# A recurrent attention kernel: the output projection of 32 tokens on four column tiles instead of 40 on two, late rows projected at the end, rows turned by VectorE

## The chip, the cores and the metric

The kernel runs on one core of a Trainium2 chip. The metric is the time of one execution in microseconds (us): a median over runs, and the span of one profiled execution, from its first to its last instruction. Engines are written as the profile writes them: PE is TensorE's matmuls, PEld its weight loads, DVE is VectorE, ACT is ScalarE, POOL is GpSimd and SP is SyncE, which here issues most of the DMAs.

## What is computed

Two independent parts share the launch and write the two halves of each output row. Part A is a sliding, dilated attention over 2048 tokens; the change does not touch its code. Part B is a recurrence over 64 segments of 32 tokens, each with 8 memory rows ahead of it:

```python
mem = mem0
for s in range(n_seg):                       # 64 segments, one after the other
    xs = x[:, s * seg_len:(s + 1) * seg_len, :]
    h = jnp.concatenate([mem, xs], axis=1)   # 8 + 32 = 40 rows of 640
    q = jnp.einsum('btd,dhe->bhte', h, Wq)   # 32 heads of 192
    k = jnp.einsum('btd,dhe->bhte', h, Wk)
    v = jnp.einsum('btd,dhe->bhte', h, Wv)
    scores = jnp.einsum('bhqe,bhke->bhqk', q, k) * scale
    p = _softmax(jnp.where(mask[None, None], scores, -1000000000.0), axis=-1)
    o = jnp.einsum('bhqk,bhke->bhqe', p, v)
    o = jnp.einsum('bhte,hed->btd', o, Wo)
    mem = o[:, :M, :]                        # the next segment's memory
    outs.append(o[:, M:, :])
```

Only the first 8 rows of a segment's output feed the next segment. The four weight matrices are 640 x 6144 in bf16, and not all of them fit on the chip.

## The kernel before, in words

**Windows.** The 40 rows of a segment are handled as 32 + 8. The *main* rows are the 8 memory rows and the first 24 tokens. The last 8 tokens, the *late* rows, need no memory, so they are projected ahead of time, for four segments at once (32 rows, called `ahead`). A DRAM tile `XW` holds, for each segment, 32 main rows and 32 ahead rows (`copy_windows`, issue at L382, 26 DMAs). `load_x` (L469) brings the window of segment s + 1 into one of two tiles `HX` with a DMA transpose, at the start of segment s; a later copy (L657) overwrites the memory rows.

**Weights.** A weight unit is a 128-row slice of 1536 columns (Wq, Wk, Wv) or of two 640-column rows (Wo). 60 units stay in SBUF (`wres_*`), 24 units per segment are streamed from DRAM copies (`wcopy_*`) through six buffers of one tile (`wstream`, L417): 8 of Wk and 6 of Wv at 384 KB, 10 of Wo at 320 KB. All these DMAs are issued by SP, in one order; a fetch waits until PE has used the unit six places before it.

**Projections.** `project32` (L485) multiplies 32 rows by a unit as four matmuls of 384 columns, one on each 32-column tile of PE, so four run abreast. There are four groups g of eight heads each. Results go through a copy to bf16 (`to_sb`, L492), a turn by PE against an identity (`turn`, L498) and copies into `QT` and `KT`. Late rows of Wq, Wk and Wv are renewed each fourth segment, one k group and one v group and one q group in each segment (`RENEW`).

**Attention.** `scores` (L575) takes 16 matmuls per group; `softmax` and `put_p` run on DVE with the exponential on ACT (L582 to L600); `turn_p` (L610, L613) turns the probabilities and `mix` (L627) multiplies by the values with 32 matmuls on four row tiles. The result is copied into `OT` (L465), 40 tokens wide.

**Output.** `project_out` (L641) multiplies 64 columns of `OT` (40 of them tokens) with 320-column halves of a Wo unit: two matmuls abreast, 96 per segment, all summed into `Y`. At the end of a segment ACT copies `Y` to bf16 (L708), PE turns the 8 memory rows (`memory_rows`, L648 and L654), DVE copies them into the next `HX` (L657), and POOL issues two output DMAs (L716).

**Order.** `segment` (L659) writes out the order of PE by hand: projections of the next group stand between a group's scores and its use. The end of a segment is a loop-carried chain: the last `project_out`, the copy of `Y`, the memory rows, the next segment's first q projection. Instructions of the other engines, SP's among them, are put in order by a scheduler when the program is built.

PSUM has eight banks: three for projections, four single ones for everything that is turned, scored or mixed (`ps_x`), one for `Y`.

Of the kernel before, what the change touches and what calls it, by code (L numbers as in the profile page):

```python
# [23 lines left out]
def part_a(ctx, tc, A_x, A_wqkv, A_wo, out, ident, emit_loads):  # L24
# [239 lines left out]
    with tc.manual_schedule(engines={mybir.EngineType.PE, mybir.EngineType.DVE, mybir.EngineType.Activation}):  # L264
# [4 lines left out]
        for b in range(-1, n_blk):  # L269
# [13 lines left out]
STREAMED = {"k": ((2, 4), (2, 4), (0, 4), (0, 4)), "v": ((0, 4), (0, 4), (2,), (2,)),  # L283
            "o": (3, 5, 7, 10, 11, 13, 17, 18, 22, 23)}
# [3 lines left out]
LEAD_IN, PAD = 114, 4  # L288
# [9 lines left out]
def part_b(ctx, tc, B_x, B_mem0, B_Wq, B_Wk, B_Wv, B_Wo, out, ident, n_seg, pre, nbuf, mid):  # L298
# [6 lines left out]
    w_in = {m: w.rearrange("(dc p) h e -> p dc (h e)", p=128) for m, w in (("q", B_Wq), ("k", B_Wk), ("v", B_Wv))}  # L305
    wo_v = B_Wo.rearrange("h e d -> (h e) d").rearrange("(i k p) d -> p i k d", p=128, k=2)

    def unit_src(u):  # L310
        m, c, dc = u
        if m == "o":
            return wo_v[:, c]
        return w_in[m][:, dc, 1536 * c:1536 * c + 1536]

    def unit_cols(u):
        return 1280 if u[0] == "o" else 1536

    copied = {}

    def copy_streamed():

        order = [(m, g) for m, g in need]
        units = []
        for m, g in order:
            if m == "o":
                units += [("o", i, 0) for i in range(6 * g, 6 * g + 6) if i in STREAMED["o"]]
            else:
                units += [(m, g, dc) for dc in range(5) if m != "q" and dc in STREAMED[m][g]]
        for u in units:  # L330
            copied[u] = dpool.tile([128, unit_cols(u)], BF16, name="wcopy_%s%d_%d" % u)[:]
            nc.sync.dma_start(unit_tile(copied[u], u), unit_src(u))
# [4 lines left out]
    for m, g in need:  # L337
        if m == "o":
            resident += [("o", i, 0) for i in range(6 * g, 6 * g + 6) if i not in STREAMED["o"]]
        else:  # L340
            resident += [(m, g, dc) for dc in range(5) if m == "q" or dc not in STREAMED[m][g]]
    res, wait = {}, set()

    def unit_tile(t, u):
        v = t[:, 0:unit_cols(u)]
        return v.rearrange("p (k d) -> p k d", k=2) if u[0] == "o" else v

    def place_resident(pool, units):
        for u in units:
            res[u] = pool.tile([128, unit_cols(u)], BF16, name="wres_%s%d_%d" % u)[:]  # L350

    def load_resident(units, engs):
        for k, u in enumerate(units):
            engs[k % len(engs)].dma_start(unit_tile(res[u], u), unit_src(u))
# [8 lines left out]
    XW = dpool.tile([n_seg, 2 * SEG, Dm], BF16, name="xwindows")  # L363

    def copy_windows():

        rows = [(XW[0, 0:M], mem2[0:M]), (XW[0, M:SEG], x2[0:SEG - M])]
        for a, b in ((1, 49), (49, n_seg)):
            rows.append((XW[a:b, 0:SEG], x2[SEG * a - M:SEG * b - M].rearrange("(s n) d -> s n d", n=SEG)))
        groups = x2.rearrange("(t n) d -> t n d", n=SEG)[:, SEG - M:SEG]  # L370
        groups = groups.rearrange("(m k) n d -> k m n d", k=4)
        windows = XW[:].rearrange("(m k) n d -> k m n d", k=4)
        for r in range(4):
            for i in range(4):
                dst = windows[r][:, SEG + M * i:SEG + M * i + M]
                if i >= r:
                    rows.append((dst, groups[i]))
                else:
                    rows.append((dst[0:n_seg // 4 - 1], groups[i][1:n_seg // 4]))
                    rows.append((dst[n_seg // 4 - 1], groups[i][n_seg // 4 - 1]))  # L380
        for dst, src in rows:
            nc.sync.dma_start(dst, src)  # L382

    def emit_loads(turn_x):
        turn_x(1)
        load_resident(resident[:n_pre], [nc.sync])
        turn_x(2)
        copy_streamed()
        return copy_windows
# [7 lines left out]
    HXs = [xpool.tile([128, 5, 64], BF16, name=f"HX{i}") for i in range(2)]  # L397
# [5 lines left out]
    qk_sb = pool("b_qk", bufs=3)  # L403
# [3 lines left out]
    ps_x = pool("b_ps_x", bufs=4, space=PSUM)  # L407
# [3 lines left out]
    wait.update(resident[n_pre + len(early):])  # L411
# [8 lines left out]
    def get_unit(u):  # L420
        if u in fetched:
            return fetched.pop(u)
        if u in res:
            if u in wait:
                wait.remove(u)
                load_resident([u], [nc.sync])
            return res[u]
        return fetch(u)
# [9 lines left out]
    PADW = 64 - L  # L438
    QT = cpool.tile([128, 12 * L + PADW], BF16, name="QT")
    KT = cpool.tile([128, 4, 4, L], BF16, name="KT")  # L440
# [3 lines left out]
    OT = cpool.tile([128, 12 * L + PADW], BF16, name="OT")  # L444
    free = [cpool.tile([128, 3, 4, M], BF16, name=f"Lb{i}") for i in range(BLOCKS)]
    late = {}
    VW = 448
# [3 lines left out]
    nc.gpsimd.memset(KT[:], 0.0)  # L451
    for t in [QT, OT]:
        nc.gpsimd.memset(t[:, t.shape[1] - PADW:], 0.0)
    for t in LV + [Vst]:
        nc.gpsimd.memset(t[:, 192:256], 0.0)
# [4 lines left out]
               "QT": (S_, S_, S_, V_), "KT": (S_, S_, S_, S_), "V": (S_, V_, V_, S_), "LV": (V_, S_, S_, V_),  # L460
# [6 lines left out]
    def load_x(s):  # L467
        if s < n_seg:
            nc.sync.dma_start_transpose(HXs[s % 2][:], XW[s])  # L469

    def main(s):
        return HXs[s % 2][:, :, 0:SEG]

    def ahead(s):
        return HXs[s % 2][:, :, SEG:2 * SEG]
# [320 lines left out]
```

## Time and profile before

| | us |
|---|---|
| runs: median (lowest to highest) | 1974.92 (1973.56 to 1977.6) |
| the profiled execution's span | 1976.8 |
| first projection of Part B (L485) starts | 171.1 |
| copy of Y (L708) of the first and of the last segment starts | 217.5 and 1970.7 |
| one segment, mean of the 63 between these | 27.83 |
| PE busy, share of the span | 96% |
| DVE, ACT, POOL busy, share of the span | 52%, 47%, 13% |

The profile's page has six parts. Part 1 gives each engine's busy time. Part 2 cuts the span into 40 slices of 49.4 us and gives busy tenths, the granted PE clock, the mean busy share of the 16 DMA engines and the GB/s moved. Part 4 is the chain of work that ended last, followed back. Part 5 lists groups of instructions with their mean duration and what the engine waited for before them. Part 6 lists DMAs by source line, with the median time from issue to landing. Matmuls run abreast and are pipelined, so the duration of one (328 ns) is not the pace: the pace is read from the starts of successive ones in the timeline.

### The profile page before, as it was taken

The numbers are of one execution on the slowest core, as the hardware profiler recorded it, in microseconds if no ns is written. First come the engines' busy times: TensorE is split into PE (matmuls) and PEld (weight loads), VectorE is DVE, ScalarE is ACT, GpSimd is POOL, SyncE is SP. The second block draws the span as 40 slices with busy tenths as digits, with TensorE's granted clock in tenths as the row PEclk, the third lists the DMA queues.
The fourth block names the chain that finished last, engine by engine and source line by source line (L and its number), as shares of the span: only waits on it lengthen the run. The fifth ranks groups of instructions, "written<-read, shape, count | busy, mean of one in ns | idle before, by whom it ended". The sixth has DMA issues, their size and how long they took to land.

```text
span 1976.8 us, 99618 instructions
## 1 busy us (share of the span) xinstructions
PE 1890.8 (96%) x43006; PEld 1221.6 (62%) x43006; DVE 1032.1 (52%) x3431; ACT 927.4 (47%) x2963; POOL 262.3 (13%) x1070
## 2 busy tenths in 40 slices
PE   8998899999999999999999999999999999999998
PEld 5665566666666666666666666666666666666665
DVE  4885454455444554455445554455445554555454
ACT  3554344444444454444444454444444444444443
POOL 2001011111111111111111111111111111111111
PEclk9999999999999999999999999999999999999999
DMA  9936999999999999999999999999999999999997
GB/s 332 298 111 227 341 324 312 327 326 326 324 321 324 322 328 315 329 319 331 326 318 322 329 330 314 325 315 316 327 328 324 327 327 315 338 325 329 315 328 262
DMA packets 278203, 621.62 MB, mean 314 GB/s; under 512 B 62089, under 2 KB 72329, under 8 KB 277449
## 3 DMA queue, kind: packets, MB, share of 16 engines
q1 hardware_dynamic: 272258, 609.17, 91.3%
q8 instruction: 337, 5.52, 1.1%
q0 software_dynamic: 5504, 6.07, 1.0%
q14 instruction: 104, 0.85, 0.1%
HBM read 602.01 MB, written 19.27 MB: 314 GB/s over the span
## 4 chain that ended last, share of the span: by engine, by line
PE 67%; DMA 17%; ACT 7%; DVE 6%; issue 2%; SPq 0%; ACTq 0%; POOL 0%; POOLq 0%; DVEq 0%
PE acc L485 31%; PE Y L641 17%; DMA t<-wcopy_k 7%; PE pt L498 7%; DMA t<-wcopy_o 6%; DMA t<-wcopy_v 4%; PE Sps L575 3%; PE pq L95 3%; PE OTps L627 3%; DVE prod L151 1%; ACT sb L712 1%; ACT OT L708 1%; PE pt L610 1%; ACT KT L513 1%; ACT t L588 1%
## 5 line engine op out<-in xcount | busy, mean ns | idle before, releaser
L485 PEld LDWEIGHTS <-HX 128*32 128x32 bf16 x19380 | 467.1, 96 | 283.8 <-issue 54.5
L641 PEld LDWEIGHTS <-OT 128*64 128x64 bf16 x6144 | 317.8, 110 | 137.0 <-ACT OT L465 25.0
L485 PE MATMUL acc<-t,HX 128*32 128x384 bf16 x4524 | 342.9, 328 | 19.0 <-DMA t<-wcopy_k 9.3
L641 PE MATMUL Y<-wres_o,OT 128*64 128x320 bf16 x3584 | 331.2, 302 | 9.9 <-DVE OT L465 5.1
L485 PE MATMUL acc<-wres_q,HX 128*32 128x384 bf16 x6460 | 333.6, 328 | 1.1 <-issue 0.7
L492 ACT CAST sb<-acc 128x384 bf16<-128x384 f32 x448 | 210.1, 478 | 152.0 <-PE acc L485 132.4
L641 PE MATMUL Y<-t,OT 128*64 128x320 bf16 x2560 | 266.7, 301 | 10.4 <-DMA t<-wcopy_o 8.8
L485 PE MATMUL acc<-wres_v,HX 128*32 128x384 bf16 x4520 | 251.7, 327 | 0.7 <-DMA wres_v<-in_B_Wv_dram 0.7
L485 PE MATMUL acc<-wres_k,HX 128*32 128x384 bf16 x3876 | 224.6, 327 | 0.3 <-DVE sb L492 0.3
L588 ACT ACTIVATE t<-t 128x160 f32<-128x160 f32 x256 | 86.4, 338 | 288.5 <-DVE t L587 284.5
L498 PE MATMUL pt<-ident,sb 128*128 128x128 bf16 x1938 | 182.4, 221 | 8.5 <-ACT KT L513 0.9
L582 DVE SCALAR_TENSOR_TENSOR t<-Sps,mask 128x160 f32<-128x160 f32 x256 | 82.9, 324 | 178.5 <-PE Sps L575 173.2
L465 ACT CAST OT<-OTps 128x120 bf16<-128x120 f32 x512 | 108.6, 266 | 140.4 <-PE OTps L627 139.2
L498 PEld LDWEIGHTS <-sb 128*128 128x128 bf16 x1938 | 109.4, 97 | 87.0 <-ACT sb L492 20.5
L590 DVE TENSOR_REDUCE sm<-t 128x4 f32<-128x160 f32 x256 | 82.0, 320 | 130.9 <-ACT t L588 130.9
L465 DVE CAST OT<-OTps 128x120 bf16<-128x120 f32 x512 | 123.7, 272 | 46.1 <-PE OTps L627 45.8
L513 ACT CAST KT<-pt 128x256 bf16<-128x256 f32 (+1 forms) x323 | 109.1, 343 | 78.6 <-PE pt L498 78.1
L517 POOL COPY KT<-Lb 64x32 bf16<-64x32 bf16 x189 | 40.0, 212 | 788.2 <-PE Sps L575 656.9
L575 PEld LDWEIGHTS <-QT 128*64 128x64 bf16 x4096 | 98.4, 112 | 59.1 <-issue 52.2
L575 PE MATMUL Sps<-KT,QT 128*64 128x40 bf16 x4096 | 113.9, 187 | 5.6 <-ACT QT L507 2.6
L657 DVE CAST HX<-pt 128x40 bf16<-128x40 f32 x63 | 12.6, 200 | 179.5 <-PE pt L654 179.5
L600 DVE TENSOR_TENSOR P<-t,sm 128x128 bf16<-128x128 f32 (+1 forms) x512 | 100.2, 237 | 11.2
(91 smaller groups left out, 2130.8 us busy)
## 6 DMA issues: line engine op xcount, KB each, us to landing
t<-wcopy_o SPq DMA_DIRECT2D x640, 320.0 KB, 4.9
t<-wcopy_k SPq DMA_DIRECT2D x512, 384.0 KB, 5.3
t<-wcopy_v SPq DMA_DIRECT2D x384, 384.0 KB, 5.3
wres_q<-in_B_Wq_dram SPq DMA_DIRECT2D x20, 384.0 KB, 7.8
wres_v<-in_B_Wv_dram SPq DMA_DIRECT2D x14, 384.0 KB, 7.9
wres_k<-in_B_Wk_dram SPq DMA_DIRECT2D x12, 384.0 KB, 7.8
wres_o<-in_B_Wo_dram SPq DMA_DIRECT2D x14, 320.0 KB, 7.1
wcopy_o<-in_B_Wo_dram SPq DMA_DIRECT2D x10, 320.0 KB, 9.6
```

What stands on the lines that cost most here:

```text
L95: nc.tensor.matmul(pq[32 * d:32 * d + 32], lhsT=wcol[:, k, t, 4 * c + d, :], rhs=xTs[s][:, k, :], start=(k == 0), stop=(k == 4), tile_posi ...
L465: (S_ if copies["n"] % 2 else V_)(dst, src)
L485: nc.tensor.matmul(ps[n][32 * j:32 * j + 32, :], lhsT=X[:, dc, :], rhs=w[:, 384 * j:384 * j + 384], start=(dc == 0), stop=(dc == 4), tile_ ...
L492: copy(sb[:], p[:])
L498: nc.tensor.matmul(pt[:, k], lhsT=sb[:, 128 * c:128 * c + 128], rhs=ident, start=True, stop=True)
L513: copy(KT[:, :, 0:3:2, n0:n1].rearrange("p j c n -> p c j n"), src)
L575: nc.tensor.matmul(Sps[64 * g2:64 * g2 + 64, a, :], lhsT=QT[:, at:at + 64], rhs=KT[:, a, ((0, 1), (3, 2))[g2][part], :], start=(n == 0), s ...
L582: nc.vector.scalar_tensor_tensor(out=t1[:], in0=Sps[:], scalar=scale, in1=mask[:].unsqueeze(1).to_broadcast([128, 4, L]), op0=ALU.mult, op ...
L588: nc.scalar.activation(t1[:], t1[:], ACTF.Exp)
L590: nc.vector.tensor_reduce(out=sm[:], in_=t1[:], axis=AX.X, op=ALU.add)
L600: nc.vector.tensor_tensor(out=P[:, k, :, at:at + hi - lo], in0=t1[:, :, lo:hi], in1=sm[:].unsqueeze(2).to_broadcast([128, 4, hi - lo]), op ...
L641: nc.tensor.matmul(Y[64 * gv:64 * gv + 64, :], lhsT=OT[:, L * c:L * c + 64], rhs=w[:, n:n + 320], start=(i == 0 and r == 0), stop=(i == 23 ...
```

## The change

- **Windows and weights by quarters.** `XW` is laid out so that a segment's window is 128 rows: four quarters of the 640 columns times 32 rows. The row order of the Wq, Wk and Wv units is changed to fit (`(j dc f)`), resident units are loaded in blocks by four DMAs of 32 partitions each, and `copy_windows` issues 104 DMAs with 160-element runs where 26 stood. `load_x` becomes a plain DMA into a single tile `XS`, and DVE turns it in 32x32 blocks into `HX` (`turn_x`, placed after `put_p(s, 0)`).
- **Output of 32 tokens.** `project_out` takes 32 tokens, and puts the two chunks of a unit and its two column halves on four column tiles. The sums of the two chunks land on different partitions and are added in a new function `close`, which also turns the memory rows with DVE. POOL issues four output DMAs and one more per segment, that of the late rows.
- **Late rows.** The late 8 tokens' attention output is copied by POOL into `OL`, stored to a DRAM tile `late_o` at the end of each segment, and projected for all 64 segments after the last one (`project_late`): 16 loads of 384 KB back into the tiles of Wq, 1536 matmuls in two passes over Wo (streamed units are fetched twice), copies, and 64 DMAs of 8 rows.
- **Smaller attention products.** q's middle chunk is kept once for each of two heads, zero elsewhere, so `scores` takes 12 matmuls instead of 16; `mix` takes 24 instead of 32; `turn_p` takes 2 for each group.
- **Copies.** q's fills are three copies, k's are one; two of four k fills move from ACT to DVE; `mix` is followed by six copies instead of four. `ps_x` is two tiles of two banks.

```diff
+    w_in = {m: w.rearrange("(j dc f) h e -> j f dc (h e)", j=4, f=32) for m, w in (("q", B_Wq), ("k", B_Wk), ("v", B_Wv))}
...
+        n = len(units)
+        for j in (0, 2, 1, 3):
+            nc.sync.dma_start(t[32 * j:32 * j + 32].rearrange("p (n c) -> p n c", n=n),
+                              w_in[m][j, :, dc:dc + n, 1536 * g:1536 * g + 1536])
...
-    XW = dpool.tile([n_seg, 2 * SEG, Dm], BF16, name="xwindows")
+    XW = dpool.tile([n_seg, 4, SEG, 2, 160], BF16, name="xwindows")
+    late_o = dpool.tile([n_seg, 128, 48 * M], BF16, name="late_o")
...
-    ps_x = pool("b_ps_x", bufs=4, space=PSUM)
+    ps_x = pool("b_ps_x", bufs=2, space=PSUM)
...
-            nc.sync.dma_start_transpose(HXs[s % 2][:], XW[s])
+            nc.sync.dma_start(XS[:], XW[s].rearrange("j n w c -> (j n) (w c)"))
+
+    def turn_x(s):
+        if s < n_seg:
+            nc.vector.transpose(HXs[s % 2][:].rearrange("p w k n -> p (w k n)"), XS[:])
...
     def scores(g):
-        Sps = ps_x.tile([128, 4, L], FP32, tag="x")
-        for n in range(8):
-            a, part = n // 2, n % 2
+        Sps = bank()[:, 0:4 * L].rearrange("p (a n) -> p a n", n=L)
+        for a in range(4):
+            nc.tensor.matmul(Sps[:, a, :], lhsT=QT[:, QW * a:QW * a + 128], rhs=KT[:, a, 1, :], start=(a == 0), stop=False)
+        for a in range(4):
             for g2 in range(2):
...
     def mix(g, PT):
-        ps = [ps_x.tile([128, 3, L], FP32, tag="x", name=f"OTps{a}") for a in range(4)]
+        ps = [banks() for _ in range(2)]
...
-        for a in range(4):
-            evacuate(OT[:, 3 * L * a:3 * L * a + 3 * L], ps[a][:].rearrange("p k n -> p (k n)"))
+        for h, (first, second) in enumerate(((S_, V_), (V_, S_))):
+            p = ps[h][:, :, 0:4 * L].rearrange("p a (k n) -> p a k n", n=L)
+            O = OT[:, 2 * h:2 * h + 2]
+            first(O[:, :, 0:3:2, :], p[:, :, 0:2, :])
+            second(O[0:64, :, 1, :], p[0:64, :, 2, :])
+            second(O[64:128, :, 1, :], p[64:128, :, 3, :])
+        nc.gpsimd.tensor_copy(OL[:, :, 12 * g:12 * g + 12].rearrange("p n c -> p c n"),
+                              OT[:].rearrange("p a k n -> p (a k) n")[:, :, 32:L])
...
-                    nc.tensor.matmul(Y[64 * gv:64 * gv + 64, :], lhsT=OT[:, L * c:L * c + 64],
-                                     rhs=w[:, n:n + 320], start=(i == 0 and r == 0), stop=(i == 23 and r == 1),
-                                     tile_position=(0, 64 * gv))
+                    t = 32 * (2 * r + gv)
+                    nc.tensor.matmul(Y[t:t + 32].rearrange("p (b c) -> p b c", b=2),
+                                     lhsT=OT[:, c // 3, c % 3, 0:32], rhs=wide(w, r, gv),
+                                     start=(i == 0), stop=(i == 23), tile_position=(0, t))
...
+    def close(s, Y):
+        Ysb = OT[:].rearrange("p a k n -> p (a k n)")[:, 0:160]
+        odd = one.tile([128, 4, L], FP32, tag="t1", name="odd")[:].rearrange("p a n -> p (a n)")
+        for b, copy in ((0, V_), (1, S_)):
+            copy(odd[64 * b:64 * b + 64], Y[64:128, 160 * b:160 * b + 160])
+        for b in range(2):
+            nc.vector.tensor_tensor(Ysb[64 * b:64 * b + 64], Y[0:64, 160 * b:160 * b + 160],
+                                    odd[64 * b:64 * b + 64], op=ALU.add)
+        if s + 1 < n_seg:
+            nc.vector.transpose(XS[:, 0:160], Ysb)
+            nc.vector.tensor_copy(HXs[(s + 1) % 2][:, 0, :, 0:M],
+                                  XS[:, 0:160].rearrange("p (k n) -> p k n", n=SEG)[:, :, 0:M])
+        for j in range(4):
+            nc.gpsimd.dma_start(out2[SEG * s:SEG * s + SEG - M, Dm + 160 * j:Dm + 160 * j + 160],
+                                Ysb[32 * j + M:32 * j + SEG])
+        nc.gpsimd.dma_start(late_o[s], OL[:].rearrange("p n c -> p (n c)"))
...
         mix(3, PT[3])
         if not last:
             gl = (s + 1) % 4
-            ql = project32([ahead(s + 1)], "q", gl, range(0, 3))
+            ql = project32([ahead(s + 1)], "q", gl, slice(0, 2))
         project_out(Y, 3)
-        Ysb = OT[:, 0:320]
-        nc.scalar.copy(Ysb, Y[:])
+        close(s, Y)
...
+    def project_late():
+        dead = [("q", g, dc) for g in range(4) for dc in range(5)]
+        O = []
+        for b in range(16):
+            t = res[dead[b]].rearrange("p (i c) -> p i c", i=4)
+            nc.sync.dma_start(t, late_o[4 * b:4 * b + 4].rearrange("i p c -> p i c"))
+            O.append(res[dead[b]].rearrange("p (n c) -> p n c", c=48))
...
+        for part in ((0, 1, 2), (3,)):
+            for i in range(24):
+                w = get_unit(("o", i, 0))
+                for r in range(2):
+                    for m in part:
+                        for gv in range(2):
+                            for j in range(4):
+                                nc.tensor.matmul(sums[2 * m + gv][32 * j:32 * j + 32, 0:320],
+                                                 lhsT=O[4 * m + j][:, :, 2 * i + r],
+                                                 rhs=w[:, 640 * r + 320 * gv:640 * r + 320 * gv + 320],
+                                                 start=(i == 0 and r == 0), stop=(i == 23 and r == 1),
+                                                 tile_position=(0, 32 * j))
+            for m in part:
+                rows = res[dead[16 + m]][:, 0:640]
+                for gv, copy in ((0, S_), (1, V_)):
+                    copy(rows[:, 320 * gv:320 * gv + 320], sums[2 * m + gv][:, 0:320])
+                for k in range(16):
+                    r0 = SEG * (16 * m + k) + SEG - M
+                    (nc.sync, nc.scalar)[k % 2].dma_start(out2[r0:r0 + M, Dm:2 * Dm], rows[M * k:M * k + M])
```

More of the change, by code (lines that the diff above doesn't have):

```diff
@@ L287 @@
 BLOCKS = 18
[L288 removed]
+LEAD_IN = 114
 def next_start(m, g, s):
@@ L450, in part_b @@
     nc.gpsimd.memset(P[:], 0.0)
[L451 to L455, printed above, removed]
+    nc.gpsimd.memset(QT[:], 0.0)
     copies = {"n": 0}
@@ L603, in turn_p @@
     def turn_p(g):
[L605 to L606 removed]
+        pt = bank()[:, 0:256].rearrange("p (l n) -> p l n", l=2)
         for late in range(2):
[L608 to L614 removed]
@@ L615, in turn_p @@
-        PT = one.tile([128, 2, 2, L], BF16, tag="PT")
-        ENGINES["PT"][g](PT[:], pt[:].rearrange("p l (h n) -> p l h n", h=2)[:, :, :, 0:L])
+            nc.tensor.matmul(pt[:, late, :], lhsT=P[:, late].rearrange("p a n -> p (a n)"), rhs=ident,
+                             start=True, stop=True)
+        PT = one.tile([128, 2, 2 * L], BF16, tag="PT")
+        ENGINES["PT"][g](PT[:].rearrange("p l (h n) -> p l h n", h=2),
+                         pt.rearrange("p l (h n) -> p l h n", h=2)[:, :, :, 0:L])
```

257 lines of the change are left out of this document (136 added, 121 removed).

## The prediction

> **What bounds the kernel now.** First the page's slices, the queue shares and the issues, then the time windows (us from the start; span; busy time and count of PE, PEld, DVE, ACT, POOL; granted PE clock, DMA share, GB/s).
>
> ```profile
> PE   8998899999999999999999999999999999999998
> DMA  9936999999999999999999999999999999999997
> q1 hardware_dynamic: 272258, 609.17, 91.3%
> t<-wcopy_o SPq DMA_DIRECT2D x640, 320.0 KB, 4.9
> t<-wcopy_k SPq DMA_DIRECT2D x512, 384.0 KB, 5.3
> HX<-xwindows SPq DMA_TRANSPOSE x64, 5.2
> ```
>
> ```profile
> 497.00:1971.00 1474.00, 1426.36 (x33792) 923.65 (x33790) 749.64 (x2728) 697.41 (x2307) 199.86 (x843) 1.00 0.95 323
> 22.00:46.00 24.00, 23.00 (x403) 15.53 (x393) 15.73 (x17) 13.11 (x24) 0.00 (x0) 1.00 1.03 400
> 1055.60:1059.60 4.00, 4.00 (x95) 2.37 (x84) 1.56 (x5) 2.30 (x6) 0.21 (x1) 1.00 1.02 387
> 1036.50:1040.50 4.00, 4.00 (x108) 2.62 (x102) 2.96 (x11) 2.40 (x11) 0.00 (x0) 1.00 0.89 290
> 1024.50:1026.50 2.00, 2.00 (x36) 1.40 (x32) 0.14 (x1) 0.17 (x2) 0.00 (x0) 1.00 0.94 216
> ```
>
> The first window holds 53 segments: 27.8 us each, of which PE is busy 26.9 (1426.36 / 53). So PE bounds each segment, at full clock. But DMA stands close behind: a segment streams 14 x 384 KB + 10 x 320 KB = 8.78 MB, and 8.78 MB in 27.8 us is most of the 323 GB/s, with the DMA engines busy 0.95 of the time. What DMA can do at most is seen where many loads are queued: 400 GB/s while the resident weights load (22 to 46 us), 387 just after a segment's start, while in mid-segment, where PE sets the pace of new fetches, it is 290, and at the segment's end, where the DMA transpose of the window runs, 216. Next, what PE waits for in that stage, and the end of a segment in the timeline (start, us, engine, line).
>
> ```profile
> PE Y L641 <- DMA t<-wcopy_o: 6.3, 16, 1.0
> PE acc L485 <- DMA t<-wcopy_v: 6.2, 12, 1.4
> PE acc L485 <- DMA t<-wcopy_k: 5.5, 13, 1.0
> ```
>
> ```profile
> 1026.52 0.43 ACT L708 CAST OT<-Y 128x320 bf16<-128x320 f32 x1 [1.84 <-PE Y L641]
> ...
> 1027.00 0.39 PE L654 MATMUL pt<-ident,OT 128*64 128x8 bf16 x6
> ...
> 1027.42 0.20 DVE L657 CAST HX<-pt 128x40 bf16<-128x40 f32 x1 [2.78 <-PE pt L654]
> ...
> 1027.73 1.00 PE L485 MATMUL acc<-wres_q,HX 128*32 128x384 bf16 x20
> ...
> 1028.55 0.50 PE L485 MATMUL acc<-wres_k,HX 128*32 128x384 bf16 x8
> ```
>
> DMA waits are 18.0 us in 53 segments, 0.34 each; all PE idle is 47.6 us, 0.9 each. The chain from the copy of Y to the next q projection takes 1.21 us. And the last two lines give the pace of four matmuls abreast: 20 in 0.82 us, so 0.164 us for four of 384 columns.
>
> **Output projection: the gain.** Its 96 matmuls of 320 columns stay 96. Two abreast, 8 take 0.56 us in the timeline (two units at 1044.97 to 1045.53), so 0.14 us a pair, 48 pairs, 6.7 us. Four abreast cost 320/384 of 0.164 = 0.137 us for four; 24 of them take 3.3 us. **-3.4 us** a segment. The moving operand is read in two runs of 160 columns instead of one of 320; no row shows that. The bounds are 0 and, if the break counts as one more matmul, 96 x 0.01 (32 short ones of mix take 0.31) = 1.0; I take 0, since the other 320 columns are the same.
>
> **Scores, mix, turns of P.** 16 scores take 0.36 to 0.43 us now and 32 mixes 0.31; 16, 32 and 10 matmuls become 12, 24 and 8. A quarter of 4 x (0.36 + 0.31) is 0.67; but half of mix's streamed columns move into wider matmuls and the full-width scores no longer pair, so between 0 and -0.7; I take **-0.5**, the turns included.
>
> **End of segment.** Chain now 1.21 us. After: DVE copies half of Y (nearest: 0.27 for the 128x120 copy; 0.3), ACT the other half, and in the built order ACT waits for DVE there (0.3), two DVE adds from PSUM (0.32 each, as L582), a DVE turn of 160 columns (no row; between 0.20 of L657 and 0.35 of L587; 0.25), the copy into HX (0.2), five handovers at 0.05: 1.95. PE fills little of it (three steps of late q, 0.5, and one turn). **+0.75**, between +0.5 and +1.0.
>
> **New waits on PE.** (a) Shorter projections cover less. From scores(3) to the turn of its P, PE now takes 3.43 us (1046.08 to 1049.51), and DVE has P ready after 3.07. Six units lie between, losing 0.14 each: 2.6 us of cover, so PE waits 0.5. (b) Before the last output group, PE waits for the copies out of mix(3): three per engine (0.3 + 0.2 + 0.2) instead of two of 0.27, and only two steps of late q (0.33) beside them instead of three (0.49): +0.25. (c) q's and half of k's fills, the window's turn and the adds go to DVE: by its counts and these rows it goes from 14.1 us a segment (749.64 / 53) to about 19. Still under the period, so it costs by latency only. Together **+0.75**, between 0 and 1.3.
>
> **The window's load.** XS is one tile, so its load waits for the end of `close`; in the built order it stands on SP behind the six prefetched weights, and DVE's turn of it stands near the head of DVE's segment, ahead of the first softmax. Queued behind that turn on DVE: in every fourth segment (k group 0 renewed) the late k copy and q's fill, in the others the first softmax. Landing: 5.2 us after issue, as HX's transposes now. In the fourth-segment case PE wants the late k rows about 3.5 us after the segment's start, and gets them at 5.2 + 0.4 (turn) + 0.55 (copy) = 6.1: 2.6 lost. In the others scores(0) ends near 4.5 and its softmax starts near 5.6, but PE has q2 and v0 (1.6 us) ahead of the next need: near 0. Mean 2.6 / 4 = 0.65, partly beside DMA waits; **+0.5**, between 0 and 2.6.
>
> **DMA.** The transposes go; a plain window (82 KB), a store of late rows (98 KB) and output pieces come: about 9.0 MB a segment. At 387 GB/s 23.3 us, at 345 (the fuller windows) 26.1. With PE at about 26 it stays behind PE; I leave its 0.34 of waits as it is.
>
> Sum: 26.9 - 3.4 - 0.5 + 0.75 + 0.75 + 0.5 + idle of today 0.9 = **25.9 us** a segment, against 27.83: -1.93 x 64 = **-123.5**.
>
> **The late pass.** 1536 matmuls, 384 steps of four at 0.137 us = 52.6. Ahead of it 15 of the 16 loads of late rows (384 KB) pass through the last segment's queue beside its weights: 15 x 393 KB at 400 GB/s = 14.7 us; PE waits for those of the first pass, about 14. After it, in two rounds, the last 16 row DMAs and their landing (2.5 us for a 10 KB piece, about 5 in two rounds, behind the first pass's 48 DMAs): PE's end to the kernel's end about 10 instead of today's 6.1: +4. **+71.** The weight loads there read 32 columns at a stride of 96 bytes. Part A has strided ones (40 bytes), at 138 ns where contiguous ones of this width take 97; its matmul steps are 216 ns long and hide that, steps of 137 would not quite: 0 to +20, I take 0.
>
> **Start.** 104 window DMAs instead of 26, at 0.59 us an issue: 61 us from 93 on, so to about 155, where SP now has the window at 116 and the first stage waits for Part A's tiles until 148. Cover is Part A, which ends near 170. **+5**, between 0 and 25 (104 x 0.87, the pace of the 26 in all, ends at 184).
>
> Total on the profiled execution: 1976.8 - 123.5 + 71 + 5 = 1929. The runs' median is 2 us below that span: **1927 us**.
>
> **Rivals.** *The window's load decides (slower).* Place: DVE's turn at the head of each segment. If it lands behind all six prefetched weights, about 6 x 384 KB at 345 GB/s = 6.8 us after the segment's start, every softmax(0) starts 2.7 us late, of which q2 and v0 cover 1.1, and the fourth-segment case loses 4.2: (4.2 + 3 x 1.6) / 4 = 2.3 instead of 0.5. The period is then 27.7, and the time 1976.8 + 76 - 8 = 2045. It decides from a mean loss of 1.2 on, where 64 segments save no more than the 76 us of the late pass and the start. For it: the six weights are issued first. Against: today's transposes land after 5.2 with four or five loads ahead. 0.14.
>
> *DMA becomes the bound at today's rates.* 9.0 MB at 335 GB/s is 26.9 us: 1976.8 - 60 + 76 = 1993. For it: a share of 0.95 already. Against: 387 and 400 where the queue is full, and the transposes at 216 go. 0.12.
>
> *PE's new waits hide and the loads run at 387.* Period 24.2: 1976.8 - 232 + 76 = 1821; up to 1877 at 25.1. For it: waits on PE and DMA cover one another. [...] 0.19.
>
> Forecast (1885 to 1970): 0.55. Range: the lower end lies within the third rival, the upper takes in DMA at 335 and a slow start: **1850 to 2005**. About 0.2% (4 us) is what a measurement can tell from no change. Faster 0.74, same 0.04, slower 0.22.
>
> **What would show it.** Right: L691 at 0.137 us a step; copies of Y about 25.9 us apart; PE idle before the P turn of group 3 and at the late k turn; about 71 us from where the last segment would have ended. Wrong: DMA waits far above 0.34 us a segment (DMA is the bound), DVE's turn waiting on XS in all segments, late steps above 0.15 us, or a first projection after 185.

## The result: 29% slower, and the profile after

The changed kernel takes 2547.24 us (median of four runs, 2539.88 to 2555.83) where the kernel before took 1974.24 beside it: a ratio of 1.290, 95% interval 1.287 to 1.293. The prediction was 1927, range 1850 to 2005: wrong in sign and far outside its range. The profiled execution's span is 2554.0 us, 577.2 above that of before (1976.8). The page's slices, where before showed almost only nines for PE, for the granted clock and for DMA:

```profile
PE   8696777777777777777777777777777777777777
PEclk9798899989998989988999999999999999998899
DMA  9939878878787877777787777788777778787793
```

PE is below nine tenths in all slices but one, its clock is below nine tenths in 10 of the 40, and DMA, which stood at 0.95, has room. So neither of the two that were close to their limits before is the bound now. The time window of the loop, as shown before (span; busy of PE, PEld, DVE, ACT, POOL; granted clock, DMA share, GB/s):

```profile
540.00:2480.00 1940.00, 1484.57 (x31864) 832.68 (x31861) 1058.28 (x3694) 689.24 (x2152) 466.41 (x1374) 0.93 0.78 260
```

Copies of Y (L699) start at 260.4 and 2480.8, so a segment takes 35.24 us instead of 27.83. Of these PE is busy 27.0 and idle 8.2; it was idle 0.9. (PE does less work than before, but part of it at a lower granted clock, 0.93 in the mean where it was 1.00, so its busy time stays near 27.) Where the 577 us came from: the loop 63 x 7.41 = 467, the start 260.4 - 217.5 = 43, the tail from the last copy of Y 73.2 - 6.1 = 67.

Before, PE's longest waits in the loop were for DMA. Now (us in total, times, longest):

```profile
PE px L545 <- ACT QT L560: 101.2, 84, 4.3
PE px L545 <- ACT OT L676: 72.8, 69, 1.6
PE px L545 <- DVE Lb L494: 43.4, 27, 2.0
```

L545 is `turn`: PE turns projected rows and waits for copies out of PSUM. One such wait, in the timeline of the changed kernel (start, us, engine, line; in brackets the idle time before it and what ended it):

```profile
1009.68 0.34 PE L545 MATMUL px<-ident,sb 128*128 128x128 bf16 x3
...
1010.47 0.51 DVE L502 STREAM_TRANSPOSE HX<-XS 128x320 bf16<-128x320 bf16 x1 [2.58 <-DMA XS<-xwindows]
...
1011.79 0.29 DVE L564 CAST QT<-px 64x128 bf16<-64x128 f32 x1
...
1012.19 0.37 ACT L560 CAST QT<-px 128x256 bf16<-128x256 f32 x1 [2.31 <-DVE QT L564]
...
1012.62 0.33 PE L545 MATMUL px<-ident,sb 128*128 128x128 bf16 x3 [2.59 <-ACT QT L560]
```

Four things stand in one chain here. DVE waits 2.58 us for the window (XS) at the head of its segment. Behind it on DVE stand q1's two middle fills (L563, L564). ACT's outer fill of the same PSUM bank (L560) waits for DVE's to end. And PE's next turn, that of k1, waits for ACT's fill, although it writes the other bank of the two-bank tile, which no one is reading (by the order of calls of `bank()`, q1's turn takes the first bank of a tile here and k1's the second). The theories that follow take one of these links each: W the window, H the handover between two engines that read one bank, C the coupling of the two banks of a tile. G is the clock, O the order of the turns with two sb buffers.

### The profile page after: what moved, and what is told of

Same layout as the page of the kernel before. It is cut to its first block, busy times and chain, and to the rows that moved or that the text cites. A ratio compares the mean times of both kernels' runs of the same rounds, so it can differ in the third digit from the quotient of the medians.

```text
span 2554.0 us, 97114 instructions
## 1 busy us (share of the span) xinstructions
PE 1955.1 (77%) x40712; PEld 1129.0 (44%) x40712; DVE 1358.8 (53%) x4434; ACT 887.8 (35%) x2673; POOL 560.3 (22%) x1637
## 4 chain that ended last, share of the span: by engine, by line
PE 40%; DVE 23%; DMA 20%; ACT 8%; issue 5%; SPq 3%; ACTq 0%; DVEq 0%
PE acc L532 17%; DMA XS<-xwindows 11%; PE Y L691 8%; PE px L545 5%; DMA t<-wcopy_o 4%; SPq L409 3%; DVE t L628 3%; PE px L622 2%; ACT QT L560 2%; PE px L668 2%; DVE mx L632 2%; PE px L618 2%; DVE QT L564 2%; PE px L653 2%; DVE QT L563 2%
## 5 line engine op out<-in xcount | busy, mean ns | idle before, releaser
L545 PE MATMUL px<-ident,sb 128*128 128x128 bf16 x1938 | 220.6, 230 | 359.3 <-ACT QT L560 117.4
L545 PEld LDWEIGHTS <-sb 128*128 128x128 bf16 x1938 | 137.0, 100 | 481.3 <-issue 264.7
L677 POOL COPY OL<-OT 128x96 bf16<-128x96 bf16 x256 | 166.6, 651 | 725.7 <-ACT OT L676 519.8
L691 PE MATMUL Y<-wres_o,OT 128*32 128x320 bf16 x3584 | 238.2, 311 | 21.9 <-DVE OT L676 17.0
L563 POOL COPY QT<-Lb 64x32 bf16<-64x32 bf16 x252 | 51.4, 204 | 890.6 <-PE px L618 890.6
L691 PE MATMUL Y<-t,OT 128*32 128x320 bf16 x2560 | 218.2, 309 | 21.5 <-DVE OT L676 14.3
L691 PEld LDWEIGHTS <-OT 128*32 128x32 bf16 x6144 | 144.1, 97 | 170.3 <-DVE OT L676 55.6
L628 DVE SCALAR_TENSOR_TENSOR t<-px,mask 128x160 f32<-128x160 f32 x256 | 83.0, 324 | 250.2 <-PE px L622 248.6
L560 ACT CAST QT<-px 128x256 bf16<-128x256 f32 (+1 forms) x260 | 96.1, 370 | 254.8 <-DVE QT L564 250.5
L708 POOL DMA_DIRECT2D out_dram<-OT x256 | 128.0, 507 | 67.4 <-DVE OT L701 61.7
L502 DVE STREAM_TRANSPOSE HX<-XS 128x320 bf16<-128x320 bf16 x64 | 32.7, 511 | 167.4 <-DMA XS<-xwindows 167.4
L674 ACT CAST OT<-px 128x160 bf16<-128x160 f32 x256 | 74.1, 289 | 123.6 <-PE px L668 122.1
L674 DVE CAST OT<-px 128x160 bf16<-128x160 f32 x256 | 82.2, 321 | 60.3 <-PE px L668 59.7
```

The lines of the kernel that those rows point to most:

```text
L545: nc.tensor.matmul(pt[:, k], lhsT=sb[:, 128 * c:128 * c + 128], rhs=ident, start=True, stop=True)
L560: copy(Q[:, :, :, n0:n1].rearrange("p j c n -> p c j n"), src)
L563: copy(Qv[0:64, :, n0:n1], src[0:64])
L628: nc.vector.scalar_tensor_tensor(out=t1[:], in0=Sps, scalar=scale, in1=mask[:].unsqueeze(1).to_broadcast([128, 4, L]), op0=ALU.mult, op1=A ...
L674: first(O[:, :, 0:3:2, :], p[:, :, 0:2, :])
L677: nc.gpsimd.tensor_copy(OL[:, :, 12 * g:12 * g + 12].rearrange("p n c -> p c n"), OT[:].rearrange("p a k n -> p (a k) n")[:, :, 32:L])
```

## The experiments

All are edits of the changed kernel unless said otherwise; "a segment" is the mean distance of the copies of Y, 35.24 us in the changed kernel. Kernels whose loop is the same text differ by up to 0.5 us a segment (35.24, 35.20, 34.72 and 35.06 below), so smaller differences are not read.

**e1_window.** The window's load waits for less.

```diff
-            nc.vector.transpose(XS[:, 0:160], Ysb)
+            nc.vector.transpose(Vst[:, 0:160], Ysb)
...
         turn_x(s + 1)
+        load_x(s + 2)
```

> The changed kernel with a window load that waits for less: close turns the memory rows in the values' tile Vst instead of XS, and the load of the next window is issued right behind VectorE's turn, one segment earlier, so that XS is full long before its turn. Theory W (the window's load decides): VectorE waits 2.6 us a segment for XS, and QT and KT fills queue behind it, so 2.6 to 5 us a segment go: 2230 to 2380 us. Theory B (PSUM of two two-bank tiles decides) and theory O (order and the two sb buffers decide): the wait for XS is beside other waits, at most 0.5 us a segment goes: 2515 to 2547 us.

2399.65 us, 32.82 a segment: -2.4, just short of what W expected. The wait for XS is a third of the loss; two thirds stay.

**e2_ring.** One tile of four banks.

```diff
+    X4 = ps_x.tile([128, 4, 512], FP32, name="px")
...
+        return X4[:, n]
```

> The changed kernel with one tile of four PSUM banks in place of two tiles of two: single banks are handed out one after the other and each is free when its own reader is done. Theory B: PE's waits ahead of turns, of P turns and of mixes (L545, L653; 5.2 us a segment more than before) are half waits for the other bank of a tile, so 2 to 3 us a segment go: 2350 to 2420 us. Theories W and O: those waits are for copies of values not yet made, at most 0.5 us a segment goes: 2515 to 2547 us.

3035.06 us, 42.80 a segment: a miss for all, and the most telling run. The same spot in its timeline:

```profile
1037.30 0.33 PE L545 MATMUL px<-ident,sb 128*128 128x128 bf16 x3 [1.11 <-DVE t L628]
1039.04 0.33 PE L545 MATMUL px<-ident,sb 128*128 128x128 bf16 x3 [1.41 <-ACT QT L560]
```

Successive turns go to successive banks, yet each stands until the readers of the bank just before are done. So in this program a write waits for the readers of its whole tile, not of its bank, and more stands in one line with the larger tile: 42.80 us a segment with one tile of four banks, 35.24 with two of two. Theory B had taken the opposite as given. It becomes theory C.

**e3_nolate.** OL's copies, the store of OL and `project_late` left out.

> The changed kernel without the late rows: the copies into OL, the store of OL and the pass at the end are left out, so the last 8 rows of each segment's output are not written. All theories: the loop of 64 segments keeps its pace and only the pass (72 us) goes: about 2475 us. Were POOL's OL copies (0.65 us each) what OT or PE waits for, the pace would fall too: under 2440 us.

2454.04 us, 34.63 a segment. The pass is what goes; the loop falls by 0.6, about the scatter named above, so POOL's copies are not the cause.

**e4_sb3_order.** The same with three sb buffers and the turns where the kernel before has them.

```diff
-    qk_sb = pool("b_qk", bufs=2)
+    qk_sb = pool("b_qk", bufs=3)
...
-        both(tq[0])
         tq[1] = project_qk(s, "q", 1)
+        both(tq[0])
         both(tk[0])
...
-        both(tq[3])
         values(s, 2)
+        both(tq[3])
```

> As the run without late rows, and in the room that is free: three sb buffers as in the kernel before (the change has two) and with them the order of the kernel before, where q's first turn stands behind the second q projection and the last q turn behind the values of group 2. Theory O: PE stood at turns for sb copies and for QT and KT fills that the shorter distance laid open, 2 to 4 us a segment go: 2220 to 2350 us. Theories W and B: the waits move and stay as long: 2440 to 2475 us.

2596.59 us, 36.80 a segment, 2.2 more than e3: neither branch. From start to start PE loses 3.7 us a segment between successive turns (2.4 in e3) and 1.9 ahead of scores (0.2): with the turns close together their waits no longer lie apart, or so it seems; that was not followed. Theory O falls.

**e5_onehand.** One engine empties a bank.

```diff
-                fill_middle(V_, 0, 32, pt[:, 1])
+                fill_middle(S_, 0, 32, pt[:, 1])
...
-        for h, (first, second) in enumerate(((S_, V_), (V_, S_))):
+        for h, (first, second) in enumerate(((S_, S_), (V_, V_))):
...
-        for b, copy in ((0, V_), (1, S_)):
+        for b, copy in ((0, V_), (1, V_)):
```

> The changed kernel where one engine alone empties a PSUM bank: q's three fills all on ACT, each half of the mix by one engine (first ACT, second DVE), both halves of odd in close by DVE. Theory H (handovers: in the changed kernel's trace ACT's QT fill waits for DVE's, ACT's OT copy for DVE's, ACT's odd for DVE's, since readers of one bank on two engines run one after the other): the turns behind them wait less, 1.5 to 3 us a segment go: 2350 to 2450 us. Theory C (banks that are coupled because two share a tile): the waits stay nearly as long, 2500 to 2547 us.

2403.61 us, 32.87 a segment: -2.4, as H expected. But the edit does two things: it ends the handover, and it takes q's middle fills off DVE, in whose queue they stood behind the wait for the window. This run does not tell the two apart; e8 does in part.

**e6_single.** e3 with four single banks, and the mix of the kernel before (which needs no pairs).

```diff
-    ps_x = pool("b_ps_x", bufs=2, space=PSUM)
+    ps_x = pool("b_ps_x", bufs=4, space=PSUM)
...
-        ps = [banks() for _ in range(2)]
+        ps = [bank()[:, 0:3 * L].rearrange("p (k n) -> p k n", n=L) for a in range(4)]
```

> As the run without late rows (2454 us), with four single PSUM banks in place of two tiles of two, and with them the mix of the kernel before (32 matmuls, four copies of one bank each, values laid out in 448 columns). Theory C: in the ring of one tile the second of two turns stood for the first one's copies although it wrote another bank, and the trace of the changed kernel shows the same inside each tile of two; with single banks 3 to 5 us a segment go: 2130 to 2260 us. Theory H: only the mix's handovers go, 1 us a segment: about 2390 us. Theory W: 2440 us.

2116.39 us, 29.30 a segment: -5.3 against e3, more than C expected. The spot of the first timeline, in e6:

```profile
1006.05 0.61 PE L542 MATMUL px<-ident,sb 128*128 128x128 bf16 x6
...
1007.19 0.51 DVE L503 STREAM_TRANSPOSE HX<-XS 128x320 bf16<-128x320 bf16 x1 [2.99 <-DMA XS<-xwindows]
...
1008.91 0.37 ACT L557 CAST QT<-px 128x256 bf16<-128x256 f32 x1 [2.64 <-DVE QT L561]
```

DVE still waits for the window (2.99) and ACT still waits for DVE (2.64); but PE does both turns in one go (x6) and walks on into q2. The chain is there, and in this segment PE is no longer tied to it. Over all segments DVE waits for the window nearly as long as in the changed kernel (the changed kernel, then e6; us in total, times, longest):

```profile
DVE HX L502 <- DMA XS<-xwindows: 167.4, 61, 8.1
```

```profile
DVE HX L503 <- DMA XS<-xwindows: 146.8, 60, 8.0
```

In every fourth segment PE still stands for it, in another place. There the late rows of k0 are projected anew, their copy on DVE stands behind the window's turn, and PE waits for that copy:

```profile
1065.08 0.51 DVE L503 STREAM_TRANSPOSE HX<-XS 128x320 bf16<-128x320 bf16 x1 [4.59 <-DMA XS<-xwindows]
...
1066.09 0.51 PE L542 MATMUL px<-ident,sb 128*128 128x128 bf16 x6 [3.39 <-DVE sb L536]
```

Between 540 and 2000 us this happens 12 times, at 1.5 to 3.4 us and 2.1 in the mean, so 0.5 a segment. In the runs whose window comes early (e1, e10, e12) PE has no such wait.

**e11_pairs_oldmix.** e6 with the two tiles of two banks put back: the mix's four copies stay, only the tiles return.

```diff
+        two = [banks() for _ in range(2)]
+        ps = [two[a // 2][:, a % 2, 0:3 * L].rearrange("p (k n) -> p k n", n=L) for a in range(4)]
```

> As the run with single banks and the earlier mix (2116 us, no late rows), but with the two tiles of two banks put back; mix, its four copies and the values' layout stay those of the kernel before. Theory C (banks of one tile are coupled): the waits of turns and P turns come back, 2350 to 2454 us. Theory M (the changed mix with its six copies and handovers was what the run with single banks took away): 2116 to 2180 us.

2413.98 us, 33.84 a segment. So of e6's 5.3 us the tiles are 4.5 and the mix with its copies 0.8. C holds, M falls. (A mix takes two whole tiles, so a bank that is left over ahead of it goes unused; that is part of the 4.5 and was not measured by itself.) What PE waits for most in e11's loop, and the windows of e11 and of e6:

```profile
PE px L546 <- ACT QT L561: 70.6, 65, 3.1
```

```profile
540.00:2000.00 1460.00, 1135.61 (x26154) 641.18 (x26156) 777.64 (x2700) 490.51 (x1499) 226.69 (x855) 0.94 0.80 264
```

```profile
540.00:2000.00 1460.00, 1253.19 (x30308) 727.40 (x30300) 884.35 (x3128) 550.29 (x1735) 265.50 (x992) 0.98 0.90 306
```

In e6 no turn waits for a QT fill. Of the 4.5 us a segment, 3.4 are idle time of PE and the rest is busy time: the same matmuls take 26.3 instead of 25.1 us, the granted clock being 0.94 in e11 and 0.98 in e6.

**e7_warm.** Filler matmuls into Y's free bank at two of the waits.

```diff
         both(tq[1])
+        keep_warm(20)
         both(tk[1])
...
+        keep_warm(10)
         both(tk[2])
```

> The changed kernel with filler matmuls of the identity into Y's free bank where PE stands longest: 20 (about 1.8 us) ahead of k1's turns and 10 (0.9 us) ahead of k2's. They do nothing useful. Theory G (stalls also halve PE's clock for 3 us behind them: 0.924 granted): the clock rises to 0.96 or more and 1 to 2.5 us a segment go: 2390 to 2480 us. Rival (the halved clock lies beside waits that end as late anyway): the clock rises, the time stays or grows by up to 0.5 us a segment: 2545 to 2580 us.

```profile
540.00:2000.00 1460.00, 1152.60 (x25600) 690.65 (x25600) 806.87 (x2819) 524.70 (x1640) 356.49 (x1052) 0.97 0.80 262
```

2536.84 us, 34.75 a segment: the granted clock of the loop rises from 0.93 to 0.97 and the time falls by 10 us, between the two expected ranges and far nearer the rival's. The pace changes by no more than the scatter. So G is not the cause of the loss; that the halved clock lies mostly beside waits that end as late anyway fits this, and is not shown wait by wait.

**e8_window_onehand.** e1 and e5 together.

> The changed kernel with both the earlier window load and one engine for each bank. If handovers and the window cost one beside the other, the gains add: 2400 us less what one engine for each bank gives by itself, 2200 to 2300 us by theory H. If they cover the same waits, about 2380 to 2400 us.

2346.99 us, 31.93 a segment: -3.3, where the two alone sum to -4.8, and the time lies between the two expected ranges. They cover partly the same waits, being links of one chain. With the window early, one engine for each bank is worth 0.9 (e8 against e1), not much above the scatter; so 1.5 of e5's 2.4 are to be had only while the window is late.

**e10_fixed.** The whole kernel with single banks, e5's fills and odd, e1's window; the mix uses 64-column tiles for the middle chunk, so that values keep 384 columns.

```diff
+                for f in ((0, 0, 128, 0, 0), (1, 128, 64, 0, 0), (1, 192, 64, 64, L), (2, 256, 128, 0, L))]
```

> The whole changed kernel, late rows included, with three repairs: four single PSUM banks, with a mix whose middle chunk goes through 64-column tiles (32 matmuls, four copies of one bank each, values in 384 columns as changed); q's fills by ACT alone and odd by DVE alone; the window's load one segment earlier. If the gains add (338 us of single banks, 200 us of the other two): 2010 us, and if the two others only covered the same waits, 2210 us. The prediction's own sum had 1927 us; what is left above it is the start (43 us found, 5 taken) and waits that no repair here touches.

```profile
540.00:2000.00 1460.00, 1334.66 (x31459) 801.61 (x31458) 832.65 (x2885) 655.23 (x2165) 443.32 (x1291) 1.00 0.94 321
```

2132.43 us, 28.36 a segment, within what was expected. 415 us of the loss are repaired, and the clock is back to 1.00 in the loop by itself. It is still 8% slower than before.

**e12_mix448.** e10 with the mix of the kernel before, and OL stored in halves for room.

> As the run with three repairs (2132 us), but the mix of the kernel before: full 128-column tiles and values laid out in 448 columns, since the mix through 64-column tiles kept PE for 3.05 us a segment and this one for 1.52 in the run with single banks. The room comes from OL, stored twice a segment in halves. If PE sets the pace, 1.5 us a segment go: 2040 us. If DMA does (0.94 busy, 321 GB/s in the loop of the run with three repairs), the pace stops near 27.5 us a segment: 2075 us, and PE's waits for wcopy tiles grow.

2138.2 us, 28.50 a segment, above both expected times: PE has 1.6 us a segment less to do in the mix and the pace is the same. First lines of PE's waits in e12's loop; the second took the place of the work (it was 11.0 in e10), while the first, the end of the segment, stood in e10 as well:

```profile
PE acc L524 <- DVE HX L698: 33.6, 51, 0.7
PE Y L684 <- DMA t<-wcopy_o: 31.1, 51, 2.6
```

**e14_cut.** e12 without five of the 24 fetches of a segment.

```diff
-            w = get_unit(("o", i, 0))
+            w = get_unit(("o", 0 if i in (5, 10, 13, 18, 23) else i, 0))
```

> As the run with the mix of the kernel before and three repairs (2138 us, 28.5 us a segment), but the loop leaves out five of the ten fetches of Wo in a segment (1.64 of 9.15 MB): the units 5, 10, 13, 18 and 23 are multiplied with the resident unit 0, so the output is not that of the reference. If the transfers are the floor, the pace falls to PE's own, 26 to 26.9 us, and the total to 1970 to 2040 us. If PE's waits on copies are what is left, the pace stays within 0.4 us of 28.5 and the total above 2110 us.

2037.6 us, 26.99 a segment. The window of the loop of e12, then of e14:

```profile
540.00:2000.00 1460.00, 1285.07 (x31333) 748.77 (x31334) 820.35 (x2877) 644.88 (x2153) 461.54 (x1338) 0.98 0.93 320
```

```profile
540.00:1900.00 1360.00, 1227.92 (x30775) 726.04 (x30774) 803.42 (x2827) 633.88 (x2122) 453.82 (x1310) 1.00 0.84 276
```

With fewer bytes the pace falls by 1.5 us and DMA's share from 0.93 to 0.84. PE's DMA waits, 0.8 us a segment in e12, are gone, and its busy time falls by as much, from 25.1 to 24.4, with the granted clock back at 1.00. So under the repaired kernel the fetches are the floor, at 320 GB/s.

**e15_after_cut** and **e16_before_cut**: the same edit in the changed kernel and in the kernel before.

> The changed kernel with the same five fetches left out and unit 0 in their place (output not that of the reference). Theory C with its handovers (turns wait for copies): the transfers lie beside longer waits, 2500 to 2547 us. If the transfers cost the changed kernel time: under 2400 us.

> The kernel before with the same five fetches left out and unit 0 in their place (output not that of the reference). Its PE is busy 26.9 of 27.8 us and its DMA engines 0.94. If PE alone bounds it, only the DMA waits go (0.34 us a segment): 1950 to 1975 us. If the transfers bound it as much as PE, some 0.7 us or more: under 1935 us.

2480.65 us (34.36 a segment, -0.9) and 1935.97 us (27.34, -0.5; 2.1% faster than before, interval 1.8 to 2.4%). Both fell between the branches. In the changed kernel transfers cost little beside the 7.4 that a segment lost; the kernel before stood at PE and DMA together: without the fetches it gains more than its DMA waits (0.34) and less than 0.7.

**The start: e13_start, e17_few_issues, e18_128rows, e19_128rows_few.** e13 is e12 with every second window copy on ACT's queue; e17 copies the ahead rows with four DMAs instead of 88; e18 loads the resident units by one DMA of 128 partitions each; e19 is e17 and e18.

```diff
-        for j in (0, 2, 1, 3):
-            nc.sync.dma_start(t[32 * j:32 * j + 32].rearrange("p (n c) -> p n c", n=n),
-                              w_in[m][j, :, dc:dc + n, 1536 * g:1536 * g + 1536])
+        for i in range(n):
+            nc.sync.dma_start(t[:, 1536 * i:1536 * i + 1536], w_plain[m][:, dc + i, 1536 * g:1536 * g + 1536])
```

> As the run with the mix of the kernel before, with every second of the 104 window copies issued by ACT's queue instead of SP's. If the 43 us by which the start grew are SP's time to issue them (77 us from the first to the last in the changed kernel's trace), the first copy of Y comes 20 to 40 us earlier than in the run beside it and the total falls by as much. If they are the transfers themselves (16,000 packets of 320 bytes), it stays within 5 us.

> The changed kernel with the ahead rows of the windows copied in plain order, four DMAs where 88 stood, the same bytes in the same runs of 320 bytes (so the late rows are those of other tokens, and the output is not the reference's). If SP's 0.75 us for each issue made the start longer, the first copy of Y comes 25 to 45 us earlier than the changed kernel's 256 us, and the total is 2500 to 2525 us. If the packets did, it stays at 250 us or later.

> The changed kernel with the resident units of Wq, Wk and Wv loaded as before, by one DMA of 128 partitions each (so with the weights' rows in the order of the kernel before, and the output not the reference's). If the DMAs of 32 partitions are slow: 25 to 50 us moves near 400 instead of 220 GB/s, Part A's second transpose is issued near 52 us instead of 76, and the first copy of Y comes 15 to 30 us before the changed kernel's 256 us (SP's 77 us of window issues still stand ahead of the first window), the total near 2525 us. If not: 250 us or later.

> The same with the windows in 20 issues as well (late rows of other tokens). If these two are the whole start, the first projection begins near 171 us as in the kernel before and the first copy of Y near 220 us, the first segment being longer by the loop's own 7 us; total near 2510 us.

The expectations' 256 us is the moment at which DVE begins to wait for the first Y; its copy starts at 260.4. e13, a miss: 2189.72 us, copy at 308.6. Half of the issues now stand on ACT, which makes copies for Part A, and Part A's last matmul ends at 255.2 where it ended at 192.2 in e12; so it says nothing of SP. e17: 2544.13 us, copy at 254.7, 5.7 earlier, so it is not the issues that made most of the start: SP's window issues shrink from 78 to 23 us, but then the first projection (196.9) waits for Part A. e18: 2497.02 us, copy at 225.1. e19: 2503.26 us, copy at 219.5, against 217.5 before. Resident loads at 25 to 50 us, before, changed, and e18, each followed by the issue of Part A's transpose behind them:

```profile
25.00:50.00 25.00, 22.66 (x381) 15.10 (x373) 17.66 (x20) 13.15 (x25) 0.00 (x0) 1.00 1.03 398
```

```profile
51.68 6.61 SPq L49 DMA_TRANSPOSE xT<-in_A_x_dram  x1
```

```profile
25.00:50.00 25.00, 22.21 (x356) 14.40 (x349) 17.22 (x19) 12.46 (x24) 0.00 (x0) 1.00 1.04 220
```

```profile
75.90 8.49 SPq L49 DMA_TRANSPOSE xT<-in_A_x_dram  x1
```

```profile
25.00:50.00 25.00, 22.67 (x376) 14.68 (x368) 18.09 (x21) 13.15 (x25) 0.00 (x0) 1.00 1.03 401
```

```profile
51.35 8.00 SPq L49 DMA_TRANSPOSE xT<-in_A_x_dram  x1
```

With 32 partitions a DMA the loads run at 220 GB/s, with 128 at 398 and 401, the DMA engines being busy all the time in each (1.03 and 1.04) and a unit's row being 1536 columns in each; Part A's third transpose on SP (the expectations call it the second) comes 24 us late and Part A with it. That is 35 of the start's 43 us, and the window issues are another 6. Why loads of 32 partitions run at little more than half the rate of those of 128 was not shown.

## Why the prediction was wrong, step by step

- **Output projection, -3.4:** right in kind, a little less in size. Four abreast come 0.14 us apart (starts at 1031.52, 1031.66, 1031.80 in the changed kernel). From each start to the next, gaps counted up to 0.2 us, the stage (L641) took 6.9 us a segment before and 3.9 in e12 (L684): -3.0.
- **Scores, mix, turns of P, -0.5:** wrong in sign. From start to start the 12 scores take 1.7 us a segment in e12 where 16 took 1.4, and the changed mix 1.3 as before.
- **End of segment, +0.75:** right. From the first copy of Y to the next q projection 1003.02 to 1005.09: 2.07 instead of 1.21, so +0.86. The order was as told, ACT behind DVE.
- **New waits on PE, "together +0.75, between 0 and 1.3":** this is the step that failed. It took each bank as free when its own copies are done and asked only how long the copies are. The change says "`ps_x` is two tiles of two banks", and the step has no term for it, so it put the price at nothing: a turn waits for the readers of the tile, so the copies of q and k came to lie in PE's path. That alone is 4.5 us a segment (e11 against e6). Into the same path came q's fills on two engines, 2.4 (e5), of which 0.9 is left once the window is early (e8 against e1); the prediction had counted one handover, at the end of the segment.
- **The window's load, +0.5, between 0 and 2.6:** near its upper end, 2.4 (e1), and for a reason that the step did not see. DVE waited for XS in nearly every segment and not in each fourth, as the sign set for "wrong" said. But it does so in e6 nearly as long (167.4 and 146.8 us in all). There, with single banks, PE stands for it mainly where the step had put the loss: in every fourth segment, at the late rows of k, for 2.1 us instead of 2.6. The forecast's +0.5 was thus right for the path it followed; the rest of the 2.4 goes with the coupled banks. No run moved the window alone with single banks, so this split is read from waits.
- **DMA, waits unchanged at 0.34:** true of the changed kernel only because it is slow. Repaired, it meets the transfers at 28.5 us a segment, above the forecast's 25.9 and above the 26.9 of the rival "DMA becomes the bound at today's rates". Without five fetches (e14) it runs at 27.0, so 1.1 above the forecast, and not because of waits: PE is idle 2.6 us a segment there, where the forecast had 2.9 (0.75 + 0.75 + 0.5 + 0.9), but it is busy 24.4 where the forecast had 23.0 (26.9 - 3.4 - 0.5). So the first two terms, the savings on PE, were 1.4 too large together (e14's mix is that of the kernel before, which takes as long as the changed one).
- **The late pass, +71:** 67 measured, right; a step took 0.136 us, and the strided weight loads (140 ns) were hidden, as taken.
- **Start, +5, between 0 and 25:** 43. The step counted the window issues (61 us, measured 78) and left out the loads that the same change cut into DMAs of 32 partitions, which SP issues ahead of Part A's transposes.

None of the four cases held the time. The slow rival named the right link, the window, at 2045; it and the forecast shared the missing term. No run shows the period of 25.1 us (1877 us) up to which the rival goes in which PE's new waits hide: the repaired loop took 28.4 and 28.5 us a segment (e10 and e12, DMA's share 0.94 and 0.93), and 27.0 with five fetches left out (e14). No repair tried here beats the kernel before: the best, e10, is at 1.080 (1.076 to 1.085). Its loop is slower by 0.5 us a segment, and its start (262.1 against 217.5) and its late pass (78.0 us from the last copy of Y against 6.1) cost it some 116 us.

What stays open: why the transfers of the loop stop at 320 GB/s when the resident loads reach 400. Fetches also wait for PE to free one of six buffers, and a run with more buffers was not made for want of room. And e4's 2.2 us were not followed turn by turn; neither was the price of the handover, apart from the queue it stands in, measured by itself.

## What to carry to other kernels

When a change regroups PSUM banks or splits the emptying of a bank over two engines, ask for each write of PE which readers it waits for (in this program those of the whole tile, not of the bank, at 4.5 us a segment in e11 against e6) and put those copies on the path before counting any saving on PE. Before taking work off a busy engine, see what stands right behind it: here a fifth of the fetches had to go before fewer matmuls showed. And a load that was cut into pieces of 32 partitions was another load here, at 220 GB/s where 128 gave 398: price such a load by a row of the same shape, with all that its queue carries behind it.

## What the runs showed of the chip that was not expected

PE's granted clock fell to 0.50 behind a wait of 2.59 us, the one shown above. Microseconds 1012 to 1017 of the changed kernel:

```profile
1012.00:1013.00 1.00, 0.38 (x7) 0.27 (x10) 0.57 (x3) 0.62 (x2) 0.00 (x0) 1.00 0.63 243
...
1014.00:1015.00 1.00, 1.00 (x16) 0.51 (x12) 0.26 (x2) 0.48 (x1) 0.00 (x0) 0.50 0.04 15
...
1017.00:1018.00 1.00, 0.61 (x20) 0.47 (x13) 0.88 (x2) 0.48 (x1) 0.44 (x3) 1.00 0.12 44
```

In windows of a quarter microsecond the clock falls to 0.50 at 1013.3, about 0.7 us after PE is back at work (1012.62), and returns to 1.00 at 1016.7, some 3.4 us after that. How long a wait has to be cannot be read here: the clock falls to 0.50 again at 1023.5, behind PE's waits of 0.35 and 1.23 us (at 1021.8 and 1023.3). In the loop of the kernel before its mean is 1.00. The resident loads' rates, 220 and 400 GB/s for 32 and 128 partitions, are told with the start.
